# V transfers issued by ScalarE on its own queue, all other transfers by SyncE

## Chip, cores and metric

One core of a Trainium2 chip. The metric is the device time of one execution in microseconds (us); lower is better. All runs quoted gave correct results. Each kernel runs several times, in alternation with the kernel before on the same chip. Single runs are marked fast or slow (slow here: over 1.5% above the fastest of the same kernel), and a ratio is computed from the fast ones only; a median is of all runs.

## The reference

A decode step for two sequences. Attention over a cache, with 32 heads and a window of 2048 positions of the cache, head size 192:

```python
q = layernorm(x) @ wq                      # (2, 32, 1, 192)
scores = einsum("bhqd,bhkd->bhqk", q, k) * 192 ** -0.5
o = einsum("bhqk,bhkd->bhqd", softmax(scores), v)
h = x + o @ wo
h2 = h + (gelu(ln(h) @ w_gate) * (ln(h) @ w_up)) @ w_down
```

Each byte of K and V is used once: about 50 MB of K, 50 MB of V, and 22 MB of weights. Hence the kernel lives from its transfers.

## The kernel before

Four (head, batch) pairs form a group; there are 16 groups. A group has two K tiles, two V tiles (1536 KB each, 128 rows of 12288 bytes) and one `wo` tile. Every fourth group also needs a `wq` tile. All go into one ring buffer in SBUF, which holds about nine tiles. `load` gives a tile its place; `pump` emits the transfer as soon as the tiles that lay there before have been used. The operations of each engine run in the order in which they were emitted.

```python
        def pump():
            while queue:
                key, off, nbytes, src, shape, i = queue[0]
                old = [q for q in live if q[1] < off + nbytes and off < q[1] + q[2]]
                if any(q[0] not in used for q in old):
                    return
                # ... (cut)
                P.op("sp", lambda e, v=v, src=src: e.dma_start(v, src), W=toks + [("sem", i % NSEM)],
                     dma=f"d{i % NSEM}")

        # order of the loads
        load_k(0); load_wq(0); load_k(1)
        for g in range(NG):
            if g > 0 and g + 1 < NG:
                if (g + 1) % 4 == 0:
                    load_wq((g + 1) // 4)
                load_k(g + 1)
            load_v(g)
            load_wo(g)
        load_ffn()

        # order of the work: group g attends while the K tiles of group g + 1 are transposed
        for g in range(NG):
            transposes(2 * g + 2); e_columns(g); o_columns(g - 1)      # (conditions cut)
            q_rows((g + 1) // 4)                                      # every fourth group, needs wq
            transposes(2 * g + 3); oproj(g - 1); q_stationary(g + 1)
            pv(g, 0); scores(g + 1); pv(g, 1); softmax(g + 1)
```

So K of group g + 1 is used before V of group g, and the loads are queued in that order. In the profile, L427 is the transposes of K, L527 the PV matmuls, L447 the projection by `wq`, L556 the projection by `wo`, L436 and L439 the copies of transposed K by ScalarE (ACT) and VectorE (DVE), L535 ScalarE's copy of the PV result, and L261 the issue of a transfer.

## Time and profile before

| | before |
|---|---|
| device time, median | 304.98 us (304.61 to 305.4, 4 runs) |
| profiled span | 303.6 us |
| data moved | 122.3 MB |

The page of the kernel before, in order: busy time of the engines; busy tenths of the DMA engines and their GB/s in 40 slices of the span; the queue, with packets, MB and share of 16 engines' time; the chain that ended last, by engine; the issues, with KB each and median us from issue to landing.

```profile
PE 235.6 (78%) x3169; PEld 190.1 (63%) x3169; DVE 130.5 (43%) x360; ACT 112.2 (37%) x138; POOL 3.2 (1%) x9
...
DMA  6999999999999999999999999999999999999980
GB/s 240 412 435 414 427 426 420 428 399 427 425 422 423 426 421 421 427 399 428 421 428 426 421 418 426 421 407 420 433 419 426 421 421 417 429 419 424 417 308 27
...
q1 hardware_dynamic: 16292, 122.30, 96.9%
...
DMA 57%; PE 31%; SPq 5%; DVE 3%; ACT 1%; issue 1%
...
ring<-in_A_k_cache_dram SPq DMA_DIRECT2D x32, 1536.0 KB, 24.2
ring<-in_A_v_cache_dram SPq DMA_DIRECT2D x32, 1536.0 KB, 24.7
ring<-in_A_wq_dram SPq DMA_DIRECT2D x4, 1920.0 KB, 23.7
```

The DMA engines are full from the second slice to the thirty-eighth, at about 422 GB/s. One tile takes about 3.7 us at that rate, but lands 24 us after its issue: some 20 us of other transfers stand ahead of it. That is the depth of the queue. K and V wait equally long, because they wait in one line.

The waits of the kernel before, with us in total, times, and the longest in us:

```profile
ACT osb L535 <- PE ops L527: 71.5, 16, 6.5
...
PE tps L427 <- DMA ring<-in_A_k_cache_dram: 33.2, 10, 7.6
```

PE loses 33 us to K tiles over the whole run. ScalarE idles 71.5 us just ahead of its copy of the PV result.

```profile
274.65 23.22 DMA ring<-in_B_w_down_dram
297.88 0.04 issue
297.92 0.97 PE m L629 x20
298.92 0.18 DVE yT L316
```

The last weights land at 297.9 us, and the result is ready 1 us later. Transfers and TensorE finish almost together.

### The profile page before, as it was taken

Reading aid. Unit: us, or ns where it says so; the run is one execution under the profiler, and the core shown is the slowest. Engines: PE = TensorE matmul, PEld = TensorE weight load, DVE = VectorE, ACT = ScalarE, POOL = GpSimd, SP = SyncE. Lnnn points to the kernel's source line nnn. Section 1 sums busy time; section 2 is a strip of 40 time slices with the busy share of each in tenths; the row PEclk is TensorE's granted clock in tenths of the full one; section 3 lists DMA queues with packets and bytes.
Section 4 is the critical chain, followed back from the end, with each engine's and each line's share of the span. In section 5 each row is a group of like instructions: output and inputs, shape, how many; then the busy total and the mean of one; then the engine's idle time right before and its main releaser. Section 6 shows DMA issues by size and latency. Waiting matters only on the chain.

```text
span 303.6 us, 7058 instructions
## 1 busy us (share of the span) xinstructions
PE 235.6 (78%) x3169; PEld 190.1 (63%) x3169; DVE 130.5 (43%) x360; ACT 112.2 (37%) x138; POOL 3.2 (1%) x9
## 2 busy tenths in 40 slices
PE   2878798962999988791898979692799889796762
PEld 1737394932868675771867676671785858575662
DVE  5837263720345364341446454351252736453120
ACT  2336343630425263522336353432243644442000
POOL 4000000000000000000000000000000000000000
PEclk9999979995798899798799999798579999998555
DMA  6999999999999999999999999999999999999980
GB/s 240 412 435 414 427 426 420 428 399 427 425 422 423 426 421 421 427 399 428 421 428 426 421 418 426 421 407 420 433 419 426 421 421 417 429 419 424 417 308 27
DMA packets 16323, 122.76 MB, mean 404 GB/s; under 512 B 1698, under 2 KB 3236, under 8 KB 7844
## 3 DMA queue, kind: packets, MB, share of 16 engines
q1 hardware_dynamic: 16292, 122.30, 96.9%
q8 instruction: 25, 0.41, 0.6%
q14 instruction: 6, 0.05, 0.0%
HBM read 122.29 MB, written 0.00 MB: 403 GB/s over the span
## 4 chain that ended last, share of the span: by engine, by line
DMA 57%; PE 31%; SPq 5%; DVE 3%; ACT 1%; issue 1%
DMA ring<-in_A_k_cache_dram 49%; PE tps L427 19%; DMA ring<-in_B_w_down_dram 8%; SPq L261 5%; PE m L541 3%; PE sps L489 3%; PE m L556 2%; PE ops L527 1%; ACT eexp L502 1%; PE m L447 1%; PE m L468 1%; PE m L539 1%; DVE mx L494 1%; DVE ktr L439 1%; PE m L512 1%
## 5 line engine op out<-in xcount | busy, mean ns | idle before, releaser
L427 PE MATMUL tps<-identf,ring 128*128 128x128 f32 x768 | 109.5, 305 | 37.4 <-DMA ring<-in_A_k_cache_dram 33.2
L427 PEld LDWEIGHTS tps<-identf,ring 128*128 128x128 f32 x768 | 101.1, 161 | 42.4 <-DMA ring<-in_A_k_cache_dram 34.0
L436 ACT ACTIVATE ktr<-tps 128x1024 bf16<-128x1024 bf16 x80 | 79.6, 1023 | 77.4 <-PE tps L427 77.4
L439 DVE COPY ktr<-tps 128x1024 bf16<-128x1024 bf16 x112 | 73.7, 688 | 47.3 <-PE tps L427 45.4
L489 PE MATMUL sps<-ktr,rq 128*32 128x512 bf16 x384 | 46.5, 631 | 0.7 <-DVE rq L316 0.5
L535 ACT ACTIVATE osb<-ops 128x384 f32<-128x384 f32 x16 | 7.9, 491 | 71.5 <-PE ops L527 71.5
L494 DVE TENSOR_REDUCE mx<-sps 128x1 f32<-128x512 f32 x16 | 11.1, 692 | 49.4 <-PE sps L489 49.4
L527 PEld LDWEIGHTS ops<-ring,ering 128*32 128x32 bf16 x1024 | 22.9, 101 | 10.5 <-issue 9.0
L527 PE MATMUL ops<-ring,ering 128*32 128x192 bf16 x1024 | 28.5, 255 | 0.2 <-DMA ring<-in_A_v_cache_dram 0.2
L489 PEld LDWEIGHTS sps<-ktr,rq 128*32 128x32 bf16 x384 | 10.9, 108 | 21.9 <-issue 21.0
L502 ACT ACTIVATE eexp<-sps,nm 128x1024 bf16<-128x1024 f32 x16 | 17.8, 1114 | 12.7 <-DVE nm L500 12.7
L541 PE MATMUL m<-sel,osb 128*128 128x2 f32 x96 | 19.4, 318 | 0.0
L541 PEld LDWEIGHTS m<-sel,osb 128*128 128x128 f32 x96 | 18.6, 269 | 0.0
L556 PEld LDWEIGHTS m<-ot,ring 128*128 128x128 bf16 x240 | 11.8, 129 | 1.1 <-DVE ot L316 1.1
L312 DVE TENSOR_SCALAR zrhs<-oh_b,zr 128x2 f32<-128x2 f32 x16 | 3.7, 229 | 20.4 <-ACT eexp L502 20.4
L556 PE MATMUL m<-ot,ring 128*128 128x2 bf16 x240 | 11.6, 177 | 0.9 <-DVE ot L316 0.9
L316 DVE TENSOR_TENSOR ering<-m,bmask 128x128 bf16<-128x128 f32 x16 | 11.3, 709 | 1.9 <-PE m L512 1.3
L498 PEld LDWEIGHTS m<-mrhs,pm 128*128 128x128 f32 x32 | 4.8, 188 | 11.5 <-DVE mrhs L312 11.5
L498 PE MATMUL m<-mrhs,pm 128*128 128x4 f32 x32 | 6.2, 263 | 7.1 <-DVE mrhs L312 7.1
L316 DVE TENSOR_TENSOR rq<-m,mask 128x24 bf16<-128x24 f32 x64 | 7.2, 175 | 9.6 <-PE m L468 9.6
L468 PE MATMUL m<-identb,qrow 2*128 2x2 bf16 x192 | 7.2, 159 | 4.6 <-DVE hT L316 3.7
L468 PEld LDWEIGHTS m<-identb,qrow 2*128 2x128 bf16 x192 | 5.8, 92 | 6.3 <-DVE hT L316 4.8
(84 smaller groups left out, 85.4 us busy)
## 6 DMA issues: line engine op xcount, KB each, us to landing
ring<-in_A_k_cache_dram SPq DMA_DIRECT2D x32, 1536.0 KB, 24.2
ring<-in_A_v_cache_dram SPq DMA_DIRECT2D x32, 1536.0 KB, 24.7
ring<-in_A_wq_dram SPq DMA_DIRECT2D x4, 1920.0 KB, 23.7
ring<-in_A_wo_dram SPq DMA_DIRECT2D x16, 480.0 KB, 19.7
ring<-in_B_w_gate_dram SPq DMA_DIRECT2D x1, 1920.0 KB, 27.4
ring<-in_B_w_up_dram SPq DMA_DIRECT2D x1, 1920.0 KB, 22.4
ring<-in_B_w_down_dram SPq DMA_DIRECT2D x3, 640.0 KB, 23.7
xrow<-in_A_x_dram SPq DMA_DIRECT2D x1, 2.5 KB
```

The lines of the kernel that those rows point to most:

```text
L261: P.op("sp", lambda e, v=v, src=src: e.dma_start(v, src), W=toks + [("sem", i % NSEM)], dma=f"d{i % NSEM}")
L316: return lambda e: e.tensor_tensor(out=out, in0=a, in1=b, op=op)
L427: ins = e.transpose(tps[bi][:, 128 * u:128 * (u + 1)], kv[:, off:off + 128], identf[:, :])
L436: act(lambda e, dst=dst, bv=bv: e.activation(out=dst, in_=bv, func=ACT.Copy), W=[("kt", slot, bank)], X=[("t", bi)])
L439: dve(lambda e, dst=dst, bv=bv: e.tensor_copy(dst, bv), W=[("kt", slot, bank)], X=[("t", bi)])
L468: ins = e.matmul(m1[:, col:col + 2], lhsT=qx[:, h, o:o + 255:2], rhs=identb[p0:p0 + 2, p0:p0 + 2], start=True, stop=True, tile_position=(p ...
L489: ins = e.matmul(sps[32 * j:32 * (j + 1), :], lhsT=rq[:, g % 2, j, k, :], rhs=r, start=(k == 0), stop=(k == 5), tile_position=(0, 32 * j))
L494: dve(lambda e: e.tensor_reduce(out=mx[:, :], in_=sps[:, :], axis=AX.X, op=ALU.max), W=["mx"], X=["s"])
L502: act(lambda e: e.activation(out=eexp[:, :].rearrange("p (x d) -> p x d", d=2), in_=sps[:, :].unsqueeze(2).to_broadcast([128, 512, 2]), fu ...
L527: ins = e.matmul(ops_[32 * r:32 * (r + 1), 192 * h:192 * (h + 1)], lhsT=ering[:, g % 2, h, t, :], rhs=vv[:, DH * t:DH * (t + 1)], start=(h ...
L541: ins = e.matmul(m1[:, 32 + 2 * kk:34 + 2 * kk], lhsT=osb[:, kk:384:3], rhs=sel[:, :], start=True, stop=True)
L556: ins = e.matmul(m1[:, 48 + 2 * c:50 + 2 * c], lhsT=wo[:, kk, c:D:NC5], rhs=ot[:, kk, :], start=(kk == 0 and c == 0), stop=(kk == 2), skip ...
```

## The change

V transfers leave SyncE's queue and are issued by ScalarE on its own queue, in the hope that two issuers keep the DMA engines better supplied.

```diff
-                P.op("sp", lambda e, v=v, src=src: e.dma_start(v, src), W=toks + [("sem", i % NSEM)],
+                P.op("act" if key[0] == "v" else "sp", lambda e, v=v, src=src: e.dma_start(v, src), W=toks + [("sem", i % NSEM)],
                      dma=f"d{i % NSEM}")
```

The place of each tile in the ring, the waits for free slots, the bytes and the work of PE, DVE and POOL stay the same.

## The prediction

> **What bounds it now.** The transfers. The page puts queue q1 at 96.9% of the span of the 16 DMA engines: 122.3 MB, about 422 GB/s in mid-run. In the chain of waits 57% is DMA, 49% of it K tiles, no V tile. PE is next: 78% busy; a group of four heads costs it 14 to 15.7 us (starts of PV matmuls in the chain: 86.7, 102.4, 116.3) against about 16.8 us of transfers (7.1 MB a group at 422 GB/s, worked out). All loads stand in one queue in ring order, K(g+1), V(g), wo(g), nearly the order of use. K needs about 24 us from issue to landing, so some 20 us of transfers is always queued.
>
> **What the change does.** It removes no bytes and no waits on buffers. 32 issues of V leave SyncE's queue and enter ScalarE's stream, where the ring slot was freed.
> - Issue cost on ScalarE: 32 at about 0.54 us (median of V issues, view of the ring tile), 17 us on an engine 37% busy. Most stand ahead of the copy of the PV result, where ScalarE idles about 4.4 us a group (waits: 71.5 us, 16 times). On the critical path: 0 to 1 us.
> - SyncE's long issues (up to 10 us[...]) shrink; this gains nothing.
> - Bandwidth: the same 16 engines. The Trainium skill, "DMA: Bandwidth & Descriptors", section "Issuing engines are not separate DMA queues", says that queues of different issuers interleave on the same engines and save only issue time. No gain.
> - Order: the same page ("Queues, rings and completion order") says that each engine alternates between its queues packet by packet. No run here shows that yet. If so, V no longer waits behind K. V(g) is issued 1 to 4 us after K(g+1) but used after it; at half the rate it lands some 10 us before its use, and the K tiles land later by that jump.
>
> **On the critical path.** V(g) is 3.1 MB, 7.4 us at 422 GB/s, plus part of V(g+1): K late by about 7 to 12 us, from the first group on. While 20 us of transfers is queued, the DMA engines stay full, so this does not add up over groups. It shows at the end: from 262.7 us (landing of the last K pair's first tile) to the last matmuls at 298.9, PE works almost without a pause; waits that could absorb lateness (V, last weights) are about 3 us. So the end moves by about 4 to 9 us.
>
> **Predicted.** 312 us, 306 to 319. Faster by over 2%: 3%; within 2%: 40%; slower by over 2%: 57%.
>
> **What would show it.** V's issue-to-landing falls to about 15 us, K's stays or grows; the first K tile lands near 11 us instead of 8, the second group's K (transposed near 23.7 and 27.5 us) at 30 to 40. PE's waits on K tiles grow from 33 us; those on V vanish. DMA share falls to about 94%, lost in the last slices. ScalarE's busy time and mean copy (1023 ns) unchanged. SP issues over 2 us become rare.
>
> **What would make it wrong.** If the engines serve the older queue first, K isn't late and the time stays within 1%. If two streams move more than 426 GB/s, a gain of 1 to 2% is possible. If PE's slack (1 to 2 us a group) takes up the lateness, the time is near 306. If ScalarE is held in an issue when a queue is full[...], its copies stop PE and the loss is larger; likewise if late PE empties the queue in mid-run.

## More of the kernel before

The end of the kernel before: TensorE's timeline in group 13 (start, us, instruction), and the last steps of the chain:

```profile
252.35 2.82 PE L427 MATMUL tps<-identf,ring 128*128 128x128 f32 x24
...
256.37 0.84 PE L527 MATMUL ops<-ring,ering 128*32 128x192 bf16 x32
```

The work from the second K tile of group 14 (252.35 us) to the result (298.92 us) takes TensorE 46.57 us.

## The result

| | before | after |
|---|---|---|
| device time, median | 304.98 us | 314.69 us (313.13, 316.22, 313.15, 316.65) |
| profiled span | 303.6 us | 311.3 us |
| ratio after/before | | 1.0317, 95% interval 1.0265 to 1.037 |

A ratio is the mean time of one kernel's fast runs over that of the other's of the same rounds, so it is not quite the ratio of the medians. All outputs are right. All four runs are marked fast, yet they fall into two times 3 us apart. The profile is of a shorter one (313.13 us).

The page after, the same lines as above:

```profile
PE 237.6 (76%) x3169; PEld 191.5 (62%) x3169; DVE 130.5 (42%) x360; ACT 111.3 (36%) x138; POOL 3.2 (1%) x9
...
DMA  7999999999999999999999999999999999999800
GB/s 267 431 414 425 415 422 429 421 406 429 423 423 422 424 419 426 416 412 420 426 419 428 423 419 430 411 414 425 425 422 423 427 417 419 418 423 416 318 23 2
...
q1 hardware_dynamic: 11684, 71.97, 55.9%
q10 hardware_dynamic: 4608, 50.33, 38.7%
...
DMA 55%; PE 34%; DVE 4%; ACT 3%; issue 1%; SPq 1%; ACTq 1%
...
ring<-in_A_v_cache_dram ACTq DMA_DIRECT2D x32, 1536.0 KB, 14.7
ring<-in_A_k_cache_dram SPq DMA_DIRECT2D x32, 1536.0 KB, 25.1
ring<-in_A_wq_dram SPq DMA_DIRECT2D x4, 1920.0 KB, 19.0
```

Engines and transfers do the same work. V now lands after 14.7 us instead of 24.7; K, no sooner than before. The rate in mid-run is the same. What is new is the end of the GB/s row: two slices of 7.8 us with almost no transfers.

The windows view of three stretches, of before and then of after (last columns: TensorE clock granted, DMA share, GB/s):

```profile
240.00:262.00 22.00, 19.54 (x310) 14.45 (x308) 10.80 (x30) 9.55 (x12) 0.00 (x0) 1.00 1.01 423
262.00:297.00 35.00, 27.20 (x459) 23.43 (x460) 11.80 (x40) 8.64 (x14) 0.00 (x0) 0.73 0.95 389
297.00:307.00 10.00, 1.24 (x24) 1.07 (x23) 0.18 (x1) 0.00 (x0) 0.00 (x0) 0.56 0.03 4
```

```profile
240.00:262.00 22.00, 16.64 (x188) 14.12 (x189) 7.95 (x21) 6.60 (x8) 0.00 (x0) 0.84 1.01 421
262.00:297.00 35.00, 29.94 (x438) 24.27 (x436) 13.66 (x38) 10.90 (x14) 0.00 (x0) 0.84 0.95 385
297.00:307.00 10.00, 7.09 (x184) 6.76 (x184) 2.75 (x15) 0.69 (x3) 0.00 (x0) 0.50 0.02 3
```

Transfers are done at the same time in both kernels: the same GB/s in each stretch, nothing after 297 us. But TensorE has run 188 matmuls instead of 310 between 240 and 262 us, and still has 184 to do after 297 us, against 24. The time is not lost by the transfers as a whole. It is lost because TensorE is behind when they end.

The waits after, and the end of the kernel as above:

```profile
ACT osb L535 <- PE ops L527: 71.8, 15, 5.7
...
PE tps L427 <- DMA ring<-in_A_k_cache_dram: 36.4, 14, 12.1
```

```profile
261.50 4.48 PE L427 MATMUL tps<-identf,ring 128*128 128x128 f32 x24 [1.59 <-DMA ring<-in_A_k_cache_dram]
...
267.19 0.85 PE L527 MATMUL ops<-ring,ering 128*32 128x192 bf16 x32
```

```profile
304.07 2.57 PE m L629 x60
306.67 0.18 DVE yT L316
```

The second K tile of group 14 is transposed at 261.50 us instead of 252.35, and TensorE was waiting for it. That is 9.15 us late.

Was this tile issued late, or held up in flight? The issue of this one tile, before and then after (last figure: us from issue to landing):

```profile
ring<-in_A_k_cache_dram SPq DMA_DIRECT2D x1, 1536.0 KB, 20.7
```

```profile
ring<-in_A_k_cache_dram SPq DMA_DIRECT2D x1, 1536.0 KB, 35.5
```

Before, it was issued at 229.7 us and landed at 250.4. After, it was issued earlier, at 225.8 us, and landed at 261.4. So it was held up in flight, by 14.8 us. Four V tiles that were issued after it (at 226.4, 227.9, 231.4 and 248.3 us) landed before it. At 3.7 us a tile, four tiles are about 15 us of transfers (an estimate).

From there to the result TensorE takes 45.17 us instead of 46.57. So 9.15 - 1.40 = 7.75 us, which is the whole difference of the two ends (306.67 - 298.92). The 1.40 us are themselves a difference. The transposes of the late tile took 4.48 us instead of 2.82, which is 1.66 us more, and the windows view shows a lower granted clock there (the 0.62 and 1.00 in the third column from the end; before, then after):

```profile
252.35:255.20 2.85, 2.85 (x31) 2.85 (x32) 2.49 (x6) 1.02 (x1) 0.00 (x0) 1.00 1.03 431
```

```profile
261.50:266.00 4.50, 4.50 (x29) 4.50 (x30) 2.60 (x4) 1.02 (x1) 0.00 (x0) 0.62 1.01 425
```

All that follows took 3.06 us less, mainly because the waits that stood there before are gone: 1.32 us for K of group 15, 0.21 us for V, and 0.94 us for the last weights.

How far TensorE is behind the kernel before, by the start of the group's first PV matmuls in TensorE's timelines:

| group | 0 | 2 | 4 | 7 | 8 | 9 | 11 | 12 | 13 | 14 | 15 |
|---|---|---|---|---|---|---|---|---|---|---|---|
| before, us | 30.60 | 61.63 | 102.28 | 155.99 | 169.96 | 184.65 | 228.51 | 242.44 | 256.37 | 270.91 | 280.67 |
| after, us | 38.99 | 67.65 | 110.13 | 157.65 | 171.63 | 192.05 | 227.01 | 247.42 | 267.19 | 281.12 | 290.51 |
| behind, us | 8.4 | 6.0 | 7.9 | 1.7 | 1.7 | 7.4 | -1.5 | 5.0 | 10.8 | 10.2 | 9.8 |

The lag comes at once, goes nearly to zero twice, and returns. It doesn't grow by the group. What counts is that it is large at the end.

### The profile page after: what moved, and what is told of

Read it like the earlier page. It is cut to its first block, busy times and chain, and to the rows that moved or that the text cites. A ratio compares the mean times of both kernels' runs of the same rounds, so it can differ in the third digit from the quotient of the medians.

```text
span 311.3 us, 7057 instructions
## 1 busy us (share of the span) xinstructions
PE 237.6 (76%) x3169; PEld 191.5 (62%) x3169; DVE 130.5 (42%) x360; ACT 111.3 (36%) x138; POOL 3.2 (1%) x9
## 3 DMA queue, kind: packets, MB, share of 16 engines
q1 hardware_dynamic: 11684, 71.97, 55.9%
q10 hardware_dynamic: 4608, 50.33, 38.7%
## 4 chain that ended last, share of the span: by engine, by line
DMA 55%; PE 34%; DVE 4%; ACT 3%; issue 1%; SPq 1%; ACTq 1%
DMA ring<-in_A_k_cache_dram 55%; PE tps L427 15%; PE sps L489 5%; PE ops L527 4%; PE m L541 3%; PE m L556 2%; ACT eexp L502 2%; PE m L468 1%; SPq L261 1%; PE m L629 1%; DVE ktr L439 1%; PE m L539 1%; PE m L447 1%; ACT osb L535 1%; PE sps L606 1%
## 5 line engine op out<-in xcount | busy, mean ns | idle before, releaser
L427 PE MATMUL tps<-identf,ring 128*128 128x128 f32 x768 | 111.6, 308 | 41.8 <-DMA ring<-in_A_k_cache_dram 36.4
L436 ACT ACTIVATE ktr<-tps 128x1024 bf16<-128x1024 bf16 x80 | 79.8, 1023 | 84.6 <-PE tps L427 81.8
L498 PEld LDWEIGHTS m<-mrhs,pm 128*128 128x128 f32 x32 | 4.8, 188 | 11.0 <-DVE mrhs L312 10.8
## 6 DMA issues: line engine op xcount, KB each, us to landing
ring<-in_A_v_cache_dram ACTq DMA_DIRECT2D x32, 1536.0 KB, 14.7
ring<-in_A_wo_dram SPq DMA_DIRECT2D x16, 480.0 KB, 17.7
ring<-in_B_w_down_dram SPq DMA_DIRECT2D x3, 640.0 KB, 13.8
```

The source lines that it names most:

```text
L427: ins = e.transpose(tps[bi][:, 128 * u:128 * (u + 1)], kv[:, off:off + 128], identf[:, :])
L436: act(lambda e, dst=dst, bv=bv: e.activation(out=dst, in_=bv, func=ACT.Copy), W=[("kt", slot, bank)], X=[("t", bi)])
```

## The experiments

Three theories. ORDER: the engines serve the two queues side by side, so V lands early and K, which is needed first, lands late. ISSUE: the 32 issues cost ScalarE time, and its copies hold up TensorE. RATE: two queues together move less than one. RATE already has the windows above against it.

Twelve runs follow, all with three timed rounds; the last repeats the changed kernel. "Ratio" is to the kernel before on the same chip, with its 95% interval.

### e1_v_first: V ahead of K in the one queue

```diff
+                load_v(g)
                 load_k(g + 1)
-            load_v(g)
+            else:
+                load_v(g)
             load_wo(g)
```

> All loads on SyncE's one queue, but V(g) stands ahead of K(g+1) in the order. ORDER (V lands ahead of K, K is late by one V pair, 7.4 us, less about 3 us of slack at the end): slower than before by 3 to 6 us, 308 to 311 us, with all transfers landed at about 298 us as before. ISSUE (ScalarE's time for issuing is the cost) and RATE (two queues move less or disturb each other): 305 us as before, since neither is present.

Measured: 312.44 and 315.18 us in the fast runs, ratio 1.0265 (1.0212 to 1.0319). Two more runs, the profiled one among them, were slow (317.2 and 317.7), so its profile isn't used. With a single queue, and no issue on ScalarE, a changed order costs about what the change costs. ISSUE and RATE expected nothing here. The two fast times are 1.4 and 4.2 us above the top of ORDER's range. One caution: in the slow run's page the transfers fall to 193 and 349 GB/s in two slices between 158 and 174 us, while SyncE's issues wait for TensorE to free places in the ring. Whether the fast runs have such a stretch too is not known. If they do, part of e1's loss may come from it.

### e2_act_time: ScalarE's time without the queue

All transfers stay on SyncE. ScalarE gets a copy at the places where the change lets it issue V, with the same waits for TensorE.

```diff
+                if key[0] == "v" and key[1] >= 2:
+                    j = key[1] % 8
+                    o2 = P.op("act", lambda e, j=j: e.activation(out=junk[:, 1 + j, :], in_=junk[:, 0, :], func=ACT.Copy),
+                              R=["junk"], W=[("junk", j)])
+                    o2.deps += [y for y in o.deps if y.dma_sem is None and y.eng == "pe"]
```

> All loads on SyncE as before; ScalarE runs a copy of about 0.5 us at 30 of the places where the changed kernel has it issue V, with the same waits on TensorE. ORDER: within 1 us of before (304 to 306). ISSUE: most of the loss is here, 310 to 315. RATE: as before.

Measured: 305.40 us, ratio 0.9989 (0.9975 to 1.0004). The first line of its page:

```profile
PE 235.5 (78%) x3169; PEld 190.9 (63%) x3169; DVE 130.3 (43%) x360; ACT 126.6 (42%) x168; POOL 3.5 (1%) x10
```

ScalarE works 14.4 us more (126.6 against 112.2) and the kernel is no slower. ISSUE falls, as far as a copy of half a microsecond stands for an issue of 0.54 us.

### e11_v_on_pool: the change without ScalarE

```diff
+                if key[0] == "v":
+                    P.op("pool", lambda e, v=v, src=src: e.dma_start(v, src), W=toks + [("psem", key[1] % 8)],
+                         dma=f"p{key[1] % 8}")
```

> The change without ScalarE: V issued by GpSimd on its queue (with its own semaphores). ORDER: V passes K just as in the changed kernel, 311 to 317 us. ISSUE: 304 to 306.

Measured: 318.67 us, ratio 1.0432 (1.0411 to 1.0452). V lands early here too:

```profile
ring<-in_A_v_cache_dram POOLq DMA_DIRECT2D x32, 1536.0 KB, 15.6
ring<-in_A_k_cache_dram SPq DMA_DIRECT2D x32, 1536.0 KB, 25.7
```

The loss is there without any issue on ScalarE. It is 1.7 us above the top of ORDER's range and about 5 us larger than with ScalarE on the same chip (313.57 us, e12 below); why was not pursued.

### e6_late_v and e7_early_v: which groups count

```diff
-                P.op("sp", ...
+                P.op("act" if key[0] == "v" and key[1] >= 26 else "sp", ...     # e6: groups 13 to 15
+                P.op("act" if key[0] == "v" and key[1] < 26 else "sp", ...      # e7: groups 0 to 12
```

> Only V of groups 13, 14 and 15 (6 tiles) on ScalarE's queue, all else on SyncE's. ORDER, and its statement that the lateness counts only at the end: K of groups 14 and 15 late as in the changed kernel, 310 to 315 us. If lateness adds up over the groups instead: about 3/16 of the loss, 306 to 307.

> The complement: V of groups 0 to 12 (26 tiles) on ScalarE's queue, the last three groups' V on SyncE's. ORDER with the end alone counting: 305 to 307.5 us. If it adds up: 312 to 314.

Measured: e6 317.02 us, ratio 1.0382 (1.0362 to 1.0402); e7 306.69 us, ratio 1.0046 (1.0029 to 1.0063). Six V tiles of the last three groups cost 11.8 us, more than all 32 did, and 2.0 us above the top of ORDER's range. The other 26 cost 1.5 us. The timeline of TensorE in e6, at the first K tile of group 14:

```profile
250.06 0.39 PE L498 MATMUL m<-mrhs,pm 128*128 128x4 f32 x2
261.06 4.58 PE L427 MATMUL tps<-identf,ring 128*128 128x128 f32 x24 [10.61 <-DMA ring<-in_A_k_cache_dram]
```

One wait of 10.61 us makes up most of the loss. This K tile was in flight for 33.2 us, as in the changed kernel (33.3); in the kernel before it was 17.7. But e6 issued it at 227.8 us and the changed kernel already at 220.7, so e6 has it 7 us later. A likely reason for the late issue is that in e6 the earlier V tiles still stand in SyncE's stream and wait there for places; this was not tested. Lateness in the earlier groups can be made good because TensorE needs less time for a group than its transfers take (before: 13.9 us from group 11 to 12 in the table above, against about 17 us for 7.3 MB at 422 GB/s, worked out). At the end nothing is left to make it good. This pair is the strongest evidence, for both the cause and the place.

### e3_k_on_act: the mirror

```diff
-                P.op("sp", ...
+                P.op("act" if key[0] == "k" else "sp", ...
```

> The mirror of the change: K is issued by ScalarE on its own queue (again 32 issues), V and the weights by SyncE. ORDER: K now jumps ahead of V; at the end no later K is left that could jump, so the last V and weights land as before and the time is within 2 us of before (303 to 307). ISSUE and RATE: as many issues and as many bytes on the second queue as in the changed kernel, so 312 to 316.

Measured: 308.38 us, ratio 1.0097 (1.0072 to 1.0122). As many issues and bytes on the second queue as in the change, for a third of the loss: this speaks against ISSUE and RATE again. But ORDER had expected 303 to 307, and it was 308. The profile points to a reason. The waits of TensorE, and the queues in the stretch from 7 to 26 us (packets, MB, share):

```profile
PE m L447 <- DMA ring<-in_A_wq_dram: 29.1, 4, 10.5
```

```profile
q10 hardware_dynamic: 568, 6.24, 78.1%
q1 hardware_dynamic: 565, 1.74, 23.0%
```

Waits for K are gone (1.0 us left), but TensorE now waits 29.1 us for `wq` and 5.0 us for V. The two queues were served packet for packet, 568 against 565. As the profile counts them, a packet of K is a row of 12288 bytes or a 4-byte write (128 and 16 of them to a tile); one of `wq` is 3072 bytes. So `wq` got 1.74 MB in the time in which K got 6.24 MB. In the changed kernel the counts are equal as well; its queues from 230 to 246 us, V in q10:

```profile
q10 hardware_dynamic: 365, 3.90, 57.7%
q1 hardware_dynamic: 365, 2.86, 42.9%
```

In e3 the transfers also run dry for a while: the share of the DMA engines is 0.86 from 56 to 62 us and 0.91 from 160 to 168 us (318 and 348 GB/s), while issues wait for TensorE to free places in the ring. The last weights land 1.6 us later than before (299.5 against 297.9 us). This is a second effect, late TensorE that starves the transfers, which none of the three theories names; how much of e3's 3 us it makes was not measured.

### Attempts at two queues without the loss: e4, e8, e9, e10, e5

If order is all, a split that keeps the order should cost nothing. Five splits were tried. None kept the time of before.

```diff
+  P.op("act" if key[0] in ("k", "v") and key[1] % 2 else "sp", ...    # e4_alternate
+  P.op("act" if key[0] in ("k", "wq") else "sp", ...                  # e8_kwq_on_act
+  if key[0] == "v" and key[1] // 2 > gate[0]: return                  # e9_v_held: gate[0] = group whose first
+                                                                      #   K tile has been transposed
+                                                                      #   (cut: V and the other loads are pumped apart)
+  eng = min(("sp", "act"), key=lambda n: sent[n])                     # e10_balanced
+  for eng, lo, m in (("sp", 0, 0), ("act", 64, 1)): ...               # e5_halves: v[lo:lo + 64] of each load
```

> Odd tiles of K and of V (32 issues) on ScalarE's queue, even tiles and weights on SyncE's: same issues and bytes on the second queue as in the changed kernel, but both queues hold K and V in turn, so no V pair jumps a K pair; at most one tile (3.7 us). ORDER: 304 to 308. ISSUE and RATE: 312 to 316.

> K and wq on ScalarE's queue, V, wo and the last weights on SyncE's. In K alone on ScalarE's queue (308.4 us) PE waited for wq (39.8 us over its idle times), which stood behind V in the longer queue. ORDER: with wq in K's queue these waits vanish and the time is 304.5 to 306.5. If another cost of the second queue made the 3 us: 307 to 309.

> Same queues as in the changed kernel (all V on ScalarE's, the rest on SyncE's), but V(g) is issued only after the first tile of K(g) has been transposed, so a pair of V has about 10 us less in which to pass K; V(g) should still land about 15 us after its issue, about when it is used. ORDER: most of the loss is gone, 304 to 309 us; not lower, because two issues now stand between copies of ScalarE and V may be a little late. ISSUE and RATE: 312 to 316, as the number of issues and the bytes of the queues are unchanged.

> Each load goes to the queue that has been given fewer bytes so far, in ring order: two queues of equal length (alternating tiles left SyncE with 72 MB against 50 MB). ORDER in the form that the longer queue lands late: no load passes another by more than about one tile (3.7 us), 304 to 308 us. If two queues as such cost time, or issues stuck in ScalarE's stream do: 309 or more.

> Every load is cut into two halves of 64 partitions, one issued by SyncE, one by ScalarE: two queues with the same bytes in the same order, and about 90 issues on ScalarE instead of 32. ORDER (now: the queues are served packet for packet, so whatever stands in the longer queue lands late): no load passes another, 304.5 to 307 us. RATE: 312 or more. ISSUE (already refuted for a stand-in of 30 copies): more than the changed kernel, over 316.

| | time, us | ratio | what was expected of ORDER |
|---|---|---|---|
| e4_alternate | 310.37 (three slow runs of 315.81 to 316.49) | no verdict | 304 to 308 |
| e8_kwq_on_act | 310.20 (one slow run of 315.87) | 1.0157 (1.0137 to 1.0177) | 304.5 to 306.5 |
| e9_v_held | 313.42 (311.88 to 314.08) | 1.0254 (1.022 to 1.0287) | 304 to 309 |
| e10_balanced | 318.46 (316.0 to 319.25) | 1.0412 (1.0363 to 1.0461) | 304 to 308 |
| e5_halves | 464.95 (453.29 to 473.37) | 1.4949 (1.4823 to 1.5076) | 304.5 to 307 |

All five expectations missed, and the misses must be told apart. With e1, e3, e6 and e11, ORDER was too low in nine of the eleven runs for which it named a range; only e2 and e7 fell inside. It has the direction, and not the size.

In e9 the cure moved the illness, and its ratio is no clear gain on the changed kernel's on the same chip (1.0254 against 1.028). At group 14 TensorE is 5.9 us behind instead of 10.2 (first PV matmuls at 276.81 us). But then the last V tile, issued late and now sharing the engines with the last weights, makes it wait:

```profile
286.23 1.47 PE L535 MATMUL ops<-ring,ering 128*32 128x192 bf16 x32
290.62 1.47 PE L535 MATMUL ops<-ring,ering 128*32 128x192 bf16 x32 [2.92 <-DMA ring<-in_A_v_cache_dram]
```

In e10 the queues are equally long in bytes (61.5 and 60.8 MB), but `wq` loses again, packet for packet, to rows four times as long:

```profile
PE tps L430 <- DMA ring<-in_A_k_cache_dram: 24.5, 8, 7.4
...
PE m L450 <- DMA ring<-in_A_wq_dram: 20.1, 3, 9.1
```

In the kernel before, TensorE's waits for `wq` come to 0.3 us, once. Two tiles in flight side by side also both land when the second would have. That much follows from equal service; how much of e10's loss it makes was not measured. And e10 runs dry as e3 did: the DMA share is 0.71 from 56 to 62 us and 0.89 from 160 to 168 us, and its last weights land 4.2 us later than before (302.1 us). What this adds to the loss was not measured either. The changed kernel has no such stretch: from the second slice to the thirty-seventh it never moves less than 406 GB/s. In e4, whose only fast run was profiled, SyncE's queue carries 72 MB against 50. Its K tiles land after 22.7 us, those on ScalarE's after 14.2. The profile of e8 fell on its slow run, so its 310 us stay without a reading; the explanation that `wq` alone had cost e3 its 3 us did not hold there.

In e5 something else happened:

```profile
DMA  8999999999999999999999999999999999999993
GB/s 197 302 249 245 251 249 252 245 241 306 251 249 254 254 270 274 269 291 304 284 273 280 284 273 288 270 313 301 293 290 298 293 280 284 276 292 280 265 261 94
```

The engines are as busy as ever, but move 267 GB/s over the span instead of 403. (Two of the four runs, 470 and 473 us, are marked slow; the ratio is of the other two, 453 and 460 us.) Here transfers of 64 partitions from two queues were slow in themselves, and e5 says nothing about order. Whether the half width or the pairing of two halves does it was not tested.

### e12_after_again: the two times

> The changed kernel unaltered, to see its two times (about 313.1 and 316.4 us) on another chip and, if the profile falls on the longer one, where the 3 us are. Guess: in the longer one a stretch of mid-run where the DMA engines have nothing queued, because late PE had not freed slots; in the shorter one none.

Measured: 313.34, 315.81, 313.06 and 313.80 us, ratio 1.028 (1.0239 to 1.032). A longer time (315.81 us) shows on another chip too, once in four, but the profile fell on a shorter run again. What makes the longer one stays open, and the guess is untested.

No version beat both kernels. The best one with a second queue, e7 (306.69 us), is still 0.5% behind the kernel before.

## Why the prediction was right, and where not

- **Time.** Predicted 312 us, 306 to 319; measured 314.69 us. Slower by over 2% had been given 57%.
- **No gain in bandwidth.** Held: 421 and 385 GB/s after, 423 and 389 before, in the same stretches. The Trainium skill, "DMA: Bandwidth & Descriptors", section "Issuing engines are not separate DMA queues", says that queues of different issuers interleave on the same engines; the trace agrees with that.
- **Issue cost on ScalarE, 0 to 1 us.** Held for the stand-in: e2 shows no cost. Mean copy 1023 ns before and after.
- **Packet-by-packet service.** The prediction took it from the section "Queues, rings and completion order" of the same page. The traces agree in so far as two busy queues got equal numbers of packets: 365 against 365, and 568 against 565. But a packet of the profile is one row or one 4-byte write, while that section means a group of descriptors. Whether the engines switch after each row or after a group is not shown.
- **V early, K late by 7 to 12 us.** V lands 14.7 us after issue, as predicted (15). The second K tile of group 14 was transposed 9.15 us later, and the trace shows that four V tiles passed it. The first transposes began at 13.8 us, where "near 11" had been said. K of the second group began at 31.0 and 35.9 us, within the predicted 30 to 40.
- **Lateness counts at the end alone.** Held: e6 and e7. Transfers are over at the same time, and the share of the DMA engines fell to 94.6% (55.9 + 38.7), where 94% had been said.
- **What absorbs it.** The slack at the end was given as about 3 us. What follows the late tile did take up 3.06 us, but its own transposes lost 1.66 us at a lower granted clock, which the prediction did not have; 1.40 us remain. That puts the prediction's middle a little low. The longer of the two times after, about 316 us, was not foreseen either.
- **Late TensorE that empties the queue in mid-run.** Named among what would make the prediction wrong. It did not happen in the changed kernel, but it did in e3 and e10.

Steps of it that were wrong, without moving the total much:

- The end was hung on the last K pair (group 15). The tile that set it was the second of group 14, at 261.50 us. From there on TensorE hardly waited.
- PE's waits on V were to vanish. They rose from 0.2 to 1.4 us. Its waits on K hardly grew (33.2 to 36.4 us, the longest from 7.6 to 12.1). It is where the waits lie that counts, not their sum.
- "Late from the first group on" is right for the first groups, but the lag is not steady: it was 1.7 us in groups 7 and 8, and gone in group 11. The prediction has no reason why it should be back at the end. That the total came out within 3 us is in this part luck.
- A group's transfers were put at 7.1 MB and 16.8 us; with 1024 bytes to the KB they are 7.3 MB and 17.2 us.
- SyncE's long issues were to become rare. Some of them still took 4 to 10 us for a pair.

## What to carry to other kernels

A queue that is kept full is also a statement of priority: what is needed first lands first. Here a stream on a second queue got an equal share of packets at once (365 against 365), and took that share from what the compute needed next; bandwidth did not grow (421 against 423 GB/s). Before splitting, ask for each tile when it is used and what would pass it, look at the packets' sizes too, and look for the loss at the end of the kernel, where lateness can no longer be made good. Look also for stretches in mid-run where the transfers run dry.

## What the Trainium skill lacked or had wrong

- "DMA: Bandwidth & Descriptors", "Queues, rings and completion order", says that engines alternate between queues packet by packet. It does not say what this does to bytes: a queue of 3072-byte rows beside one of 12288-byte rows got 1.74 MB against 6.24 MB (565 and 568 packets as the profile counts them, single rows and 4-byte writes).
- The same page, "Issuing engines are not separate DMA queues", says that issuing from several engines saves issue time. It lacks the price: the landing order changes. Here the ratio was 1.0317 with the same bytes at the same rate.
- The same page, "Rules for kernel authors", advises against two transfers to disjoint partition halves because they serialize. Here halves from two queues were far worse than whole tiles one after the other: 267 GB/s against 403, ratio 1.4949.
